# Top-k attention followed by an ELU feed-forward: the first eight steps laid out again (mask, weight tiles, pairs of keys, first sums)

## The chip, the cores and the metric

The kernel runs on one core of a Trainium2 chip. A core has a matrix engine (TensorE, PE in the profile, with PEld for its weight loads), a vector engine (VectorE, DVE), an activation engine (ScalarE, ACT), a general engine (GpSimd, POOL) and a queue engine that issues transfers (SyncE, SP). Each works through its own instructions in order, and they wait for each other by semaphores. The metric is the device time of one execution in microseconds (us), as the median of several runs.

## The reference

Two parts follow each other: attention that keeps the 32 largest scores of each row, and a feed-forward with ELU. All is fp32. The weights of the feed-forward come as fp64 and are turned to fp32 on the chip.

```python
B, H, S, D = 8, 8, 576, 64
scores = (1 / sqrt(D)) * q @ k.transpose(0, 1, 3, 2)
kth = np.partition(scores, -32, axis=-1)[..., -32:-31]
scores = np.where(scores >= kth, scores, -1e9)
scores = scores - scores.max(-1, keepdims=True)
attn = np.exp(scores)
attn = attn / (attn.sum(-1, keepdims=True) + 1e-9)
x = (attn @ v).transpose(0, 2, 1, 3).reshape(4608, 512)
h = x @ w_in                                  # 512 x 2048
g = np.where(h > 0, h, np.exp(np.minimum(h, 0)) - 1)
out = g @ w_out                               # 2048 x 512
```

## The kernel before, in words

**Steps.** The attention is cut into 144 steps. A step takes 128 queries (a tile of tokens) of one batch and one pair of heads; the 64 rows that are left over in each batch are done two pairs at a time. Four steps make up one full tile of tokens, so steps 0 to 3 are the first tile, 4 to 7 the second. Within a step VectorE finds the 32nd largest score of each row: four rounds of "the eight largest" (`first_max`, L336, and `next_max`, L348), with three replacements between them (L342) that put the found ones out of the way, each for two heads. This is the *selection*.

**Around the selection**, for the steps before and after it:
- `transpose_qk` (L261): a pair's keys and queries are transposed on TensorE (L268, L276) and copied from the accumulators by ScalarE (L273, L281) to a tile `kq`. `load_qk` (L216) brings the pair in by SP's queue, `keep_kq` (L283) writes the transposed pair to memory, and `load_kq` (L287) reads it back for later steps. There are 32 pairs, numbered through the batches; pairs 0 to 3 belong to batch 0.
- `scores` (L294): two halves of products on TensorE (L311), each copied by ScalarE (L331).
- the mask: in early steps (`mask_early`, L364) one tiny operation on VectorE (`field`, L374), four on GpSimd (L377 to L381), two Relus on ScalarE (L386), two subtractions on GpSimd (L389) and then `neg` (L355); in later steps (`mask`, L357) three GpSimd operations for each head (L360 to L362).
- `exp` (L392): two exponentials on ScalarE (L398) that also sum each row.
- `trans` (L427): the result is transposed on TensorE (L438, L456) and copied by ScalarE (L443, L457); `attend` (L459) multiplies by the values on TensorE (L471), and after a tile's last step ScalarE copies the sums out (L481).
- `sums` and `invert` (L403 to L425): after a tile's last step, three small operations on VectorE (L407 to L409) turn the sums over, and six transfers on SP's queue spread them over the partitions; then `normalise` (L483) multiplies on GpSimd (L486).

**The feed-forward** of finished tiles is cut into pieces, which `feed` hands to TensorE between the steps (L506 and L530), with ScalarE (L520 to L522) and GpSimd (L523) in between. How much it hands out follows from a list of due steps. What is left after step 143 runs alone at the end.

**The weights.** Both weight matrices come as 32 tiles of 128 x 512 fp64 numbers. `load_weights` brings them into borrowed places (L175): tiles of the feed-forward's `g`, spare tiles, and the part of `w_out` not yet written. `split_weight` does two ScalarE operations (L185, L186), `join_weight` two on VectorE (L191, L192) and an addition on GpSimd (L196). `weight_slot` (L203) does, for slot i, the join of tile i-2, the loads that may now be issued, and the split of tile i. `decode(n, place)` says at which places of step n there is a slot. Places 1, 3 and 5 lie in the middle of a round, between replacements and maxima; 2, 4 and 6 lie after the maxima. Two slots run ahead of step 0, four in each step, and six in steps 4 and 5, so that the last joins fall into step 6.

**The order** is written out by hand: the engines get their instructions in the order in which the loop over n calls these functions, with a step's own selection (`now`), the mask, exponentials and products of the step before (`last`), and the scores of steps to come. Steps 0 to 5 are *early*. There the mask of the step before is called first, at the start of step n; the scores of step n+2 in steps 0 to 3 and those of both 6 and 7 in step 4. At the end of step 3 three pairs (4, 5, 6) are transposed, at the end of step 4 two (7, 8), at the end of step 5 one (9), and from then on one in every second step. The sums of the first tile are called after place 4 of step 4, with a call of `load_weights`.

Of the kernel before, what the change touches and what calls it, by code (L numbers as in the profile page):

```python
# [61 lines left out]
def kernel(  # L62
# [81 lines left out]
    loads = [(0, 3, "g", -1), (3, 1, "raw", -1), (4, 3, "g", -1), (7, 1, "raw", -1)]  # L144
    loads += [(8, 4, "w", -1), (12, 4, "w", -1), (16, 3, "g", 2), (25, 1, "raw", -1)]
    loads += [(26, 1, "raw", -1), (27, 1, "raw", 3), (19, 3, "g", 6)]
    loads += [(28, 1, "raw", 7), (22, 3, "w", 15), (29, 1, "raw", 25)]
    loads += [(30, 1, "raw", 26), (31, 1, "raw", 27)]
    places_in_w_out = {8: 0, 12: 8, 22: 10}

    turn = [0]

    def load_weights(most=NW, margin=1):

        while loads and most > 0 and (
# [4 lines left out]
            if home == "w":  # L160
                at = places_in_w_out[i]
                t = w_out[:, at : at + 2 * n, :].bitcast(U32)
                t = t.rearrange("p (c f) d -> p c (f d)", f=2)
            elif home == "g":
                t = gpool.tile([P, n, 2 * WN], U32, tag="g", name="raw")[:]
            else:
                t = spare_tile(1 + turn[0] % 4, "raw")[:, 0 : 2 * WN].bitcast(U32)
                t = t.rearrange("p (c n) -> p c n", c=1)
                turn[0] += 1
# [46 lines left out]
    def load_qk(b, hp):  # L216

        first = b == 0 and hp < 3
        aside = (b, hp) in ((0, 1), (0, 2), (1, 1), (1, 2), (2, 0))
# [273 lines left out]
    def ffn_pieces(blk):  # L493
# [31 lines left out]
        def project(s, part):  # L525
# [11 lines left out]
            if part == 7:  # L537
# [11 lines left out]
                max(f // 4 * NC + NC - 1, 18 if f < NG else 21),  # L549
# [74 lines left out]
    def decode(n, place):  # L624

        if place in ((1, 2, 3, 4, 5, 6) if n in (4, 5) else (3, 4, 5, 6)):
            weight_slot()
# [8 lines left out]
    extra = {3: (4, 5, 6), 4: (7, 8), 5: (9,)}  # L636
    fetch = {2: (4, 5, 6), 3: (7, 8), 4: (9,), 5: (10,)}
    for p, pair in enumerate(pairs):
        if p >= NHP:
            n = next((n for n in extra if p in extra[n]), None)  # L640
            if n is None:
                n = EARLY + 1 + 2 * (p - 10)
                turns[n] = pair
            at(n + 1, keep_kq, *pair)
        elif p >= 2:
            at(p - 1, keep_kq, *pair)

    direct = {n: (n + 2,) for n in range(NHP)}
    direct[NHP] = (EARLY, EARLY + 1)
# [4 lines left out]
    for b in range(1, B):  # L654
        for hp, n in enumerate((-5, -4, 2, 2)):
            at(first[b] + n, load_v, b, hp)

    with tc.manual_schedule():
# [17 lines left out]
        for n in range(NS + 4):  # L676
# [7 lines left out]
            if early:  # L684
                if last:
                    mask_early(last)
                if n + 2 < NHP:
                    transpose_qk(0, n + 2)
                for m in direct.get(n, ()):
                    hp = m % NHP  # L690
                    steps[m].kq = {hp: kqT[0, hp]}
                    for half in range(2):
                        scores(steps[m], half)
# [11 lines left out]
            if n in turns:  # L705
                transpose_qk(*turns[n])
            if n >= EARLY and n + 2 in turns:
                load_qk(*turns[n + 2])
            if now and n > 0:
                first_max(now)  # L710
            if last and not early:
                biases(last, early)
                mask(last, 0)
            if early:
# [9 lines left out]
                feed(n, 0.5)  # L724
                next_max(now, (n, 3))
                decode(n, 4)
                if last and last.ends:
                    load_weights(margin=0)
                    sums(last)
# [16 lines left out]
            if last:  # L746
                mask(last, 1)
                exp(last, 0)
# [50 lines left out]
```

## Time and profile before

| what | value |
|---|---|
| median of 3 runs | 1663.88 us (1662.92 to 1664.91) |
| the profiled execution | 1664.04 us, span 1662.3 us |
| busy: PE, DVE, POOL, ACT | 1571.1, 1455.5, 1142.7, 925.7 us |
| start of step 1, 2, 3, 4 on VectorE (first L336) | 26.25, 42.62, 57.69, 72.79 us |
| start of step 5, 6, 7, 8 | 96.29, 118.04, 134.42, 144.07 us |

```profile
span 1662.3 us, 28290 instructions
## 2 busy tenths in 40 slices
PE   5559999999999999999999999999999999999999
...
DVE  6889999999999999999999989979989989987000
...
PEclk7579999999999999999999999999999999999999
DMA  9853555444453513121212321221222312210000
```

Each character is one slice of 41.6 us: the busy share in tenths, for PEclk the TensorE clock that was granted, for DMA the mean busy share of the transfer engines. The first three slices are the stretch that the change touches. In the last three VectorE has no work left, and TensorE does what remains of the feed-forward.

### The profile page before, as it was taken

The page shows a single profiled execution, that of the slowest core. Times are in us where ns is not written, and L with a number is a line of the kernel's source. Part 1 is how long each engine was busy: PE and PEld are TensorE (multiplying, and loading weights), DVE is VectorE, ACT ScalarE, POOL GpSimd, SP SyncE. Part 2 cuts the span into 40 slices and gives each one's busy share as a digit, 9 for nine tenths or more (in the row PEclk, how much of TensorE's full clock was granted, in tenths as well). Part 3 has the DMA queues.
Part 4 walks back from the last instruction along what each step waited for, and adds up shares of the span by engine and source line. Part 5 has one row for each costly group of instructions (what it writes and reads, how often), then busy time and mean ns, then how long its engine had stood idle before and what let it go on. Part 6 is the DMA issues. An engine that isn't in the chain of part 4 may idle for free.

```text
span 1662.3 us, 28290 instructions
## 1 busy us (share of the span) xinstructions
PE 1571.1 (95%) x9792; PEld 1046.9 (63%) x9792; DVE 1455.5 (88%) x3070; ACT 925.7 (56%) x1887; POOL 1142.7 (69%) x1457
## 2 busy tenths in 40 slices
PE   5559999999999999999999999999999999999999
PEld 3346777777776775757566566566556566566565
DVE  6889999999999999999999989979989989987000
ACT  6666665656665564646465476466456466355121
POOL 3567777777777786878778678668668668668021
PEclk7579999999999999999999999999999999999999
DMA  9853555444453513121212321221222312210000
GB/s 316 243 192 117 166 182 154 151 127 142 143 169 93 190 46 110 65 84 70 85 70 100 112 88 61 77 85 64 91 70 100 112 59 90 77 42 8 26 7 13
DMA packets 138895, 174.49 MB, mean 105 GB/s; under 512 B 94208, under 2 KB 102400, under 8 KB 138752
## 3 DMA queue, kind: packets, MB, share of 16 engines
q1 hardware_dynamic: 135200, 171.80, 32.3%
q8 instruction: 78, 1.28, 0.3%
q10 hardware_dynamic: 3552, 0.89, 0.3%
q14 instruction: 65, 0.53, 0.1%
HBM read 144.18 MB, written 28.46 MB: 104 GB/s over the span
## 4 chain that ended last, share of the span: by engine, by line
PE 60%; DVE 24%; POOL 5%; issue 4%; ACT 4%; DMA 2%; SPq 1%; ACTq 0%; POOLq 0%; DVEq 0%
PE ops L530 21%; PE hps L506 19%; DVE m L348 11%; DVE wk L342 10%; PE scps L311 7%; PE avps L471 6%; PE eps L438 5%; DVE m L336 2%; POOL sc L362 1%; POOL gT L523 1%; PE qkps L268 1%; ACT sc L398 1%; POOL wk L360 1%; POOL wk L361 1%; DMA rb<-recd 1%
## 5 line engine op out<-in xcount | busy, mean ns | idle before, releaser
L348 DVE MAX8 m<-wk 128x8 f32<-128x576 f32 x864 | 609.5, 747 | 0.0
L506 PE MATMUL hps<-xT,w_in 128*128 128x128 f32 (+2 forms) x2432 | 531.4, 373 | 10.4 <-ACT gT L521 5.8
L530 PE MATMUL ops<-w_out,gT 128*128 128x512 f32 x1152 | 519.6, 596 | 7.6 <-ACT osb L539 7.6
L506 PEld LDWEIGHTS hps<-xT,w_in 128*128 128x128 f32 x2432 | 381.1, 192 | 134.8 <-issue 17.7
L342 DVE MATCH_REPLACE8 wk<-m,wk 128x576 f32<-128x576 f32 x576 | 423.4, 743 | 0.0
L362 POOL TENSOR_TENSOR sc<-sc,wk 128x576 f32<-128x576 f32 x278 | 392.6, 1412 | 23.3
L398 ACT ACTIVATE sc<-sc,neg 128x576 f32<-128x576 f32 x288 | 224.0, 778 | 251.0 <-POOL sc L362 245.1
L530 PEld LDWEIGHTS ops<-w_out,gT 128*128 128x128 f32 x1152 | 209.6, 190 | 240.9 <-issue 213.8
L523 POOL TENSOR_TENSOR gT<-gT,n 128x384 f32<-128x384 f32 (+1 forms) x168 | 187.6, 1124 | 178.2 <-ACT n L522 174.2
L360 POOL TENSOR_SCALAR wk<-sc,nth 128x576 f32<-128x576 f32 x278 | 208.0, 748 | 27.0
L311 PE MATMUL scps<-kq 64*128 64x288 f32 (+3 forms) x1344 | 187.1, 428 | 31.2 <-ACT kq L273 20.7
L342 DVE MATCH_REPLACE8 wk<-m,sc 128x576 f32<-128x576 f32 x288 | 211.7, 743 | 0.0
L336 DVE MAX8 m<-sc 128x8 f32<-128x576 f32 x288 | 201.2, 740 | 11.3 <-ACT sc L331 11.1
L331 ACT COPY sc<-scps 128x576 f32<-128x576 f32 x288 | 170.0, 639 | 73.8 <-PE scps L311 71.9
L361 POOL TENSOR_SCALAR wk<-wk 128x576 f32<-128x576 f32 x278 | 185.7, 668 | 23.0
L443 ACT COPY et<-eps 128x1024 f32<-128x1024 f32 x144 | 144.5, 1003 | 90.6 <-PE eps L438 89.7
L471 PE MATMUL avps<-et,vE 128*64 128x128 f32 (+1 forms) x3200 | 179.6, 268 | 5.3 <-ACT et L443 5.3
L471 PEld LDWEIGHTS avps<-et,vE 128*64 128x64 f32 x3200 | 161.7, 139 | 32.3 <-issue 24.8
L438 PEld LDWEIGHTS eps<-ident,sc 128*128 128x128 f32 x1152 | 135.3, 142 | 72.3 <-issue 36.6
L438 PE MATMUL eps<-ident,sc 128*128 128x128 f32 x1152 | 153.2, 276 | 21.8 <-ACT sc L398 19.6
L311 PEld LDWEIGHTS scps<-kq 64*128 64x128 f32 (+1 forms) x1344 | 104.6, 180 | 103.1 <-issue 31.3
L520 ACT ACTIVATE n<-hps 128x384 f32<-128x384 f32 (+1 forms) x168 | 90.3, 537 | 108.8 <-PE hps L506 102.8
(66 smaller groups left out, 927.6 us busy)
## 6 DMA issues: line engine op xcount, KB each, us to landing
kq<-kqd SPq DMA_DIRECT2D x152, 576.0 KB
kqd<-kq SPq DMA_DIRECT2D x32, 576.0 KB
rb<-recd SPq DMA_DIRECT2D x64, 128.0 KB
out_dram<-osb SPq DMA_DIRECT2D x32, 256.0 KB
kin<-in_k_dram SPq DMA_DIRECT2D x27, 256.0 KB
qin<-in_q_dram SPq DMA_DIRECT2D x26, 256.0 KB
w_out<-in_moe_w_in_dram SPq DMA_DIRECT2D x2, 2048.0 KB
vE<-in_v_dram SPq DMA_DIRECT2D x32, 128.0 KB
```

The costliest lines, as they stand in the source:

```text
L311: nc.tensor.matmul(ps[rows, j, at : at + keys.stop - keys.start], u.kq[hp][r, 1, q0 : q0 + g.ql], u.kq[hp][r, 0, keys], start=True, stop=True,
L336: nc.vector.max(u.m1[:, i, :], u.sc[:, i, :])
L342: nc.vector.match_replace(u.wk[:, i, :], u.m[:, i, :], u.cur[:, i, :], TAKEN)
L348: nc.vector.max(u.m[:, i, :], u.cur[:, i, :])
L360: nc.gpsimd.tensor_scalar(pen, s, u.nth[:, i : i + 1], 2.0**100, ALU.add, ALU.mult)
L362: nc.gpsimd.tensor_tensor(s, s, pen, ALU.add)
L398: nc.scalar.activation(s, s, AF.Exp, bias=u.neg[:, i : i + 1], scale=scale, accum_out=g.den[:, at : at + 1],)
L438: nc.tensor.transpose(ps[:, i, c * P : (c + 1) * P], e[:, k0 + c * P : k0 + (c + 1) * P], ident[:],)
L471: nc.tensor.matmul(g.av[r, hp, 0:ql], vE[g.b, hp][:, i, (c + i) % (J + 1), :], u.et[:, at, q0 : q0 + ql], start=(c == 0), stop=(c == J),)
L506: nc.tensor.matmul(ps[:, f % G, :], w_in[:, i, f * P : (f + 1) * P], blk.xT[:, i, 0:N], start=(i == 0), stop=(i == NC - 1),)
L523: nc.gpsimd.tensor_tensor(g, g, n, ALU.subtract)
L530: nc.tensor.matmul(blk.o[:], blk.gT[f // NG][:, f % NG, s * P : (s + 1) * P], w_out[:, f, :], start=(f == 0), stop=(f == NF - 1),)
```

## The change

It does five things, all in the first eight steps:
- **The mask** of an early step is called at the end of that step's selection, ahead of its last join (place 6) and of any transposes there, instead of at the start of the step after. Step 5, too, now has the early kind of mask.
- **Weight tiles:** five slots in steps 4 and 5 instead of six (place 1 falls out), so that the last two joins fall into step 7. The list of loads and their places is another: more single tiles, tiles 21, 23, 25 and 27 in places of `w_out`, each spare tile named.
- **Pairs of keys:** one pair is transposed in a step, pairs 4, 5, 6 at the ends of steps 3, 4, 5, then pairs 7 to 11 in steps 7 to 11, then one in every second step. Each pair is loaded just after the pair before it was transposed, always to the same two buffers.
- **Scores** of step n+2 are called in each of the steps 0 to 5.
- **The first tile's sums** are called after place 2 of step 4, ahead of the third round, instead of after place 4, ahead of the fourth; the call of `load_weights` beside them is gone.

```diff
-    loads = [(0, 3, "g", -1), (3, 1, "raw", -1), (4, 3, "g", -1), (7, 1, "raw", -1)]
-    loads += [(8, 4, "w", -1), (12, 4, "w", -1), (16, 3, "g", 2), (25, 1, "raw", -1)]
-    loads += [(26, 1, "raw", -1), (27, 1, "raw", 3), (19, 3, "g", 6)]
-    loads += [(28, 1, "raw", 7), (22, 3, "w", 15), (29, 1, "raw", 25)]
-    loads += [(30, 1, "raw", 26), (31, 1, "raw", 27)]
-    places_in_w_out = {8: 0, 12: 8, 22: 10}
+    loads = [(0, 3, "g", -1), (3, 1, 1, -1), (4, 3, "g", -1), (7, 1, 2, -1)]
+    loads += [(8, 4, "w", -1), (12, 4, "w", -1), (16, 2, "g", 2), (20, 1, 1, 3)]
+    loads += [(18, 2, "g", 6), (22, 1, 2, 7), (24, 1, 3, -1), (26, 1, 4, -1)]
+    loads += [(21, 1, "w", 12), (23, 1, "w", 13), (25, 1, "w", 14), (27, 1, "w", 15)]
+    loads += [(28, 1, 1, 20), (29, 1, 2, 22), (30, 1, 3, 24), (31, 1, 4, 26)]
+    places_in_w_out = {8: 0, 12: 8, 21: 8, 23: 10, 25: 12, 27: 14}
...
-                t = spare_tile(1 + turn[0] % 4, "raw")[:, 0 : 2 * WN].bitcast(U32)
+                t = spare_tile(home, "raw")[:, 0 : 2 * WN].bitcast(U32)
...
-        aside = (b, hp) in ((0, 1), (0, 2), (1, 1), (1, 2), (2, 0))
+        aside = (b, hp) in ((0, 1), (0, 2))
...
-                max(f // 4 * NC + NC - 1, 18 if f < NG else 21),
+                max(f // 4 * NC + NC - 1, 17 if f < NG else 19),
...
-        if place in ((1, 2, 3, 4, 5, 6) if n in (4, 5) else (3, 4, 5, 6)):
+        if place in ((2, 3, 4, 5, 6) if n in (4, 5) else (3, 4, 5, 6)):
...
-    extra = {3: (4, 5, 6), 4: (7, 8), 5: (9,)}
-    fetch = {2: (4, 5, 6), 3: (7, 8), 4: (9,), 5: (10,)}
     for p, pair in enumerate(pairs):
         if p >= NHP:
-            n = next((n for n in extra if p in extra[n]), None)
-            if n is None:
-                n = EARLY + 1 + 2 * (p - 10)
-                turns[n] = pair
+            n = p - 1 if p < NHP + 3 else p
+            n = n if n < EARLY + 5 else EARLY + 5 + 2 * (n - EARLY - 5)
+            turns[n] = pair
             at(n + 1, keep_kq, *pair)
...
-    direct = {n: (n + 2,) for n in range(NHP)}
-    direct[NHP] = (EARLY, EARLY + 1)
...
+    coming = [turns[n] for n in sorted(turns)]
+
+    def load_next():
+        if coming:
+            load_qk(*coming.pop(0))
...
             if early:
-                if last:
-                    mask_early(last)
                 if n + 2 < NHP:
                     transpose_qk(0, n + 2)
-                for m in direct.get(n, ()):
-                    hp = m % NHP
-                    steps[m].kq = {hp: kqT[0, hp]}
-                    for half in range(2):
-                        scores(steps[m], half)
+                ahead = steps[n + 2]
+                ahead.kq = {hp: kqT[0, hp] for hp in ahead.hps}
+                for half in range(2):
+                    scores(ahead, half)
...
-            if n in turns:
+            if n in turns and not early:
                 transpose_qk(*turns[n])
-            if n >= EARLY and n + 2 in turns:
-                load_qk(*turns[n + 2])
+                load_next()
             if now and n > 0:
                 first_max(now)
-            if last and not early:
+            if last and n > EARLY:
                 biases(last, early)
                 mask(last, 0)
...
                 if last:
                     trans(last)
                 feed(n, 0.5)
+                if last and last.ends:
+                    sums(last)
                 next_max(now, (n, 3))
                 decode(n, 4)
-                if last and last.ends:
-                    load_weights(margin=0)
-                    sums(last)
                 if last:
                     attend(last)
                 next_max(now, (n, 5))
-                decode(n, 6)
                 if last and last.ends:
                     normalise(last.g)
-                for p in extra.get(n, []):
-                    transpose_qk(*pairs[p])
-                for p in fetch.get(n, []):
-                    load_qk(*pairs[p])
+                mask_early(now)
+                decode(n, 6)
+                if n in turns:
+                    transpose_qk(*turns[n])
+                if n >= NHP - 2:
+                    load_next()
                 continue
...
             if last:
-                mask(last, 1)
+                if n > EARLY:
+                    mask(last, 1)
                 exp(last, 0)
```

Built, the orders of VectorE, ScalarE, GpSimd, TensorE and SP differ from those before in steps 0 to 10 alone, but for the places of later pairs and their transfers.

More of the change, by code (lines that the diff above doesn't have):

```diff
@@ L137, in weight @@
         return w_out[:, i - NF, :]
-    loads = [(0, 3, "g", -1), (3, 1, "raw", -1), (4, 3, "g", -1), (7, 1, "raw", -1)]
-    loads += [(8, 4, "w", -1), (12, 4, "w", -1), (16, 3, "g", 2), (25, 1, "raw", -1)]
-    loads += [(26, 1, "raw", -1), (27, 1, "raw", 3), (19, 3, "g", 6)]
-    loads += [(28, 1, "raw", 7), (22, 3, "w", 15), (29, 1, "raw", 25)]
-    loads += [(30, 1, "raw", 26), (31, 1, "raw", 27)]
-    places_in_w_out = {8: 0, 12: 8, 22: 10}
-    turn = [0]
+    loads = [(0, 3, "g", -1), (3, 1, 1, -1), (4, 3, "g", -1), (7, 1, 2, -1)]
[4 more added lines that the diff above has]
+    places_in_w_out = {8: 0, 12: 8, 21: 8, 23: 10, 25: 12, 27: 14}
     def load_weights(most=NW, margin=1):
@@ L166, in load_weights @@
             else:
-                t = spare_tile(1 + turn[0] % 4, "raw")[:, 0 : 2 * WN].bitcast(U32)
+                t = spare_tile(home, "raw")[:, 0 : 2 * WN].bitcast(U32)
                 t = t.rearrange("p (c n) -> p c n", c=1)
-                turn[0] += 1
             if i < NF:
```

## The prediction

> **What bounds the kernel now.** I read first how busy the engines are in stretches of 20 us. Columns: stretch, its length, busy time (and instructions) of PE, weight load, VectorE (DVE), ScalarE (ACT), GpSimd (POOL), then TensorE's clock, DMA share, GB/s.
>
> ```profile
> 80.00:100.00 20.00, 12.81 (x68) 9.01 (x69) 12.49 (x29) 16.61 (x31) 12.64 (x12) 0.67 0.72 236
> 100.00:120.00 20.00, 11.00 (x82) 9.80 (x80) 17.67 (x29) 11.98 (x22) 14.05 (x16) 0.76 0.43 145
> 140.00:160.00 20.00, 17.35 (x88) 9.76 (x88) 20.00 (x43) 11.83 (x25) 16.24 (x21) 1.00 0.14 33
> 240.00:260.00 20.00, 20.00 (x142) 13.43 (x142) 19.93 (x44) 13.34 (x28) 15.74 (x19) 1.00 0.45 132
> ```
>
> From 140 on VectorE is full, and from 240 TensorE too: there is nothing to win there but an earlier start. Before that VectorE stands still, and the timeline of VectorE says for whom (start, duration, instruction, then the idle time before it and who ended it):
>
> ```profile
> 63.24 1.15 DVE L191 TENSOR_SCALAR w_in<-w_in 128x512 uint32<-128x512 uint32 x1
> 75.57 0.41 DVE L191 TENSOR_SCALAR w_out<-w_out 128x512 uint32<-128x512 uint32 x1
> 87.60 0.43 DVE L191 TENSOR_SCALAR w_out<-w_out 128x512 uint32<-128x512 uint32 x1 [7.31 <-ACT w_out L185]
> 107.28 0.54 DVE L191 TENSOR_SCALAR w_out<-w_out 128x512 uint32<-128x512 uint32 x1 [2.27 <-ACT w_out L185]
> ```
>
> In step 4 a join waits 7.31 us for ScalarE's split, in step 5 2.27 us. The chain of waits shows what held ScalarE up in step 4 (start, us, what):
>
> ```profile
> 73.20 0.90 ACT kq L273
> 74.14 1.98 PE qkps L268 x8
> 76.15 1.02 ACT kq L273
> 77.21 1.98 PE qkps L268 x8
> 79.22 1.02 ACT kq L273
> 80.28 4.53 PE scps L311 x16
> 84.84 0.64 ACT sc L331
> 85.48 1.52 ACT sc L398 x4
> 87.00 0.56 ACT w_out L185
> ```
>
> Three pairs are transposed in turn, TensorE and ScalarE waiting for each other, then two steps' scores, then the exponentials, and only then the split. Last, the mask and its surroundings:
>
> ```profile
> 45.30 1.63 ACT L386 ACTIVATE wk<-sc,pos,nth 128x576 f32<-128x576 f32 x2 [2.29 <-POOL pos L381]
> 49.42 0.78 ACT L398 ACTIVATE sc<-sc,neg 128x576 f32<-128x576 f32 x1 [1.44 <-POOL neg L355]
> 99.25 5.49 PE L506 MATMUL hps<-xT,w_in 128*128 128x128 f32 x24 [1.36 <-POOL xT L486]
> ```
>
> **Does a gain before 144 us reach the end?** From step 8 (144.07) to step 80 VectorE's steps are 9.6 to 10.3 us, with a few up to 11.2, and scores are copied 16 to 28 us before VectorE reads them. The orders of all five engines are the same there but for one pair of keys, transposed a step or two later. So the start of step 8 is what counts; later steps shift with it. TensorE has 26.5 us idle between the starts of steps 4 and 11, into which a shift of some 10 us fits.
>
> **The change, part by part.** Step starts before (first L336): 26.25, 42.62, 57.69, 72.79, 96.29, 118.04, 134.42, 144.07 for steps 1 to 8. VectorE's prices: two maxima 1.33 (26.25 to 27.58), two replaces 1.44 (27.58 to 29.02), so a bare step is 4 x 1.33 + 3 x 1.44 = 9.64; a join 0.93 (75.57 to 76.50); sums 0.56 (91.03 to 91.59); field 0.08. ScalarE's: a split 1.13 (53.47 to 54.60); the two relus 1.53 (45.30 to 46.83); from the first copy of a pair to the end of the exponentials behind it 5.54 (30.48 to 36.02). Below S is the start of a step on VectorE.
>
> *Mask sooner, steps 1 to 3.* The field now stands ahead of the last join, at S-1.0. GpSimd's small operations take 0.94 (44.36 to 45.30), with 0.2 to notice; the relus start at S+0.15, not S+2.7 (45.30 against 42.62), end at S+1.7, and the split that was ahead of them ends at S+2.8. L389 and L355 need 4.1 after the relus' start (45.30 to 49.42), so the exponentials start at S+4.3, not S+6.8. In steps 2 and 3 this covers the wait of 0.55 for a split, and L389 is over at S+3.9, before the first join at S+5.5, which beside it took 1.15 and not 0.41: 0.55 + 0.74 = 1.3 less, twice. Step 1 has a pair to copy: exponentials end at S+2.8+5.54 = S+8.35 (before, S+9.8), so the late join goes from S+12.84 to S+11.4: 1.4 less. Sum -4.0. If no wait goes, 0; if all of step 1's does, -5.2. The join's add (L196) now queues behind the mask on GpSimd; only a weight load far behind waits for it.
>
> *Step 4: one pair, one step's scores, five tiles, sums sooner.* Two pairs (6.16, from 73.06 to 79.22) and one step's scores (2.2, from 82.62 to 84.84) leave the chain. ScalarE: S+2.8, then 5.54: exponentials end at S+8.35. VectorE gets to the sums after 1.33 + 1.44 + 1.33 + 0.93 = 5.03 and waits 3.3 there: the change puts a new wait one round ahead of where the sums stood before. Behind it stand all of VectorE's later rounds; later splits (ending S+9.5 and S+11.9) are then in time. Step: 9.64 + 5 x 0.93 + 0.56 + 0.08 + 3.3 = 18.25 against 23.50: -5.25. With TensorE at full clock throughout (eight scores 1.24, not 2.29) -6.3; with exponentials at S+11, -2.6.
>
> *Step 5: five tiles.* GpSimd has the normalise (1.27, L486) ahead of the mask's operations, as before: relus 1.1 later, exponentials end at S+9.45. TensorE ends the scores at S+3.9+3.3 (30.48 to 33.81) = S+7.2, then the 24 L506 at 5.49, eight transposes 1.7: S+14.4. ScalarE: copies 1.07, L520 to L522 1.49, half a split 0.57: S+17.55. Before, two splits stood ahead of this; now one does, so the fourth join, due at S+11.1, waits 6.45. Step: 9.64 + 4.65 + 0.08 + 6.45 = 20.8 against 21.75: -0.95. Ends: L506 at full clock (20 took 2.40) -3.5; two more us of lag +1.1.
>
> *Step 6.* Four joins as before, but the selection's late mask (six operations on GpSimd, L360 to L362) is replaced by the early one, over before the first join. Of 3.0 us by which joins were stretched beside GpSimd (16.38 - 9.64 - 4 x 0.93), I keep 0.9: 14.3, -2.1; ends 0 and -3.0.
>
> *Step 7.* Two joins that were elsewhere: 1.86, and 0.4 of stretch: +2.3; ends +1.9 and +4.0 (each beside an add, as at 132.71: 1.78 for 0.68).
>
> *At nothing.* Loads: four more issues on SP (0.34 to 0.55 each); tiles 28 to 31 are asked for two to five slots ahead. The last load before took 3.43 and held ScalarE 4.60 with VectorE full; cover gone, it costs that. Pairs at steps 8 to 11 are loaded one step ahead, not two: four issues take 2.85 (152.15 to 155.00), landing at most 4.5 (the first load of q), 7.4 against a step of 9.6; cover gone, 1 to 3 us of TensorE, with scores 18 us ahead. I take 0, worst +2.
>
> Sum: -4.0 - 5.25 - 0.95 - 2.1 + 2.3 = **-10.0**. The profiled execution took 1664.04 (span 1662.3), the median is 1663.88: **1654.0**.
>
> [...]
>
> **Rivals.** (1) *Slower: ScalarE stays late and the early sums wait for it.* One mechanism, at L407 in step 4 and the fourth join in step 5. For it: exponentials ended at S+14.1 in step 4 before and ScalarE was busy 16.61 of 20 there. Against: 8.4 us of that chain are gone. If they end at S+14.1 in both steps, step 4 is 14.1 + 9.9 = 24.0, step 5 20.8 + 4.65 = 25.4, the mask gains nothing in steps 1 to 3 and 6, step 7 keeps +2.3: 1664.0 + 0.5 + 3.7 + 2.3 = 1670.5. It decides from 5 us more lag in each of both steps. (2) *Hidden: TensorE holds the time.* For it: 20.00 of 20 from 240 on, so an earlier VectorE could only stand further behind. Against: its waits before 173, one of 9.2 at 121.66 and 3.6 in step 10. Then 1661 to 1664. (3) *Waits only change place:* step 4 as at exponentials S+11, step 5 and 6 unchanged, the mask half: -2.0 - 2.6 + 2.3 = -2.3, 1661.7.
>
> **How the numbers follow.** Forecast 0.72, (1) 0.10, (2) 0.08, (3) 0.10. Without (1), the sums' ends are put together so that not all go one way: 1648 to 1662, which leaves out (1), part of (2), and a little below. What a measurement can tell from no change is about 0.2%, 3.3 us, so 1660.6 to 1667.2 is "same". Faster: 0.72 and a third of (2) and (3), 0.78; slower: most of (1), 0.09; same 0.13.
>
> **What would show it.** Right: step 8 starts near 134; VectorE waits some 3 us at L407 in step 4 and some 6 at the fourth join of step 5, for ScalarE both times; no join of steps 2 and 3 above 0.5 for L191; step 7 near 12. Wrong: a wait of 8 at L407, step 8 earlier and the end not, or a load that ends ScalarE's wait in step 6.

## The result and the profile after

The kernel after takes 1660.83 us in the median of 20 runs (1659.07 to 1663.1), the kernel before on the same chip 1663.59 (1660.33 to 1666.02): a ratio of 0.9985, 95% interval 0.9978 to 0.9992. It is faster, by some 2.5 us where 10 were forecast. The profiled execution after has a span of 1659.9 us, against 1662.3 before. A line number after is that of before less 3.

Step lengths on VectorE, in us, from one first maximum to the next, against the forecast:

| step | before | after | change | forecast |
|---|---|---|---|---|
| 0, with its start | 26.25 | 26.83 | +0.6 | 0 |
| 1, 2, 3 | 16.37, 15.07, 15.10 | 15.46, 13.72, 13.71 | -3.65 | -4.0 |
| 4 | 23.50 | 19.92 | -3.6 | -5.25 |
| 5 | 21.75 | 21.30 | -0.45 | -0.95 |
| 6 | 16.38 | 14.10 | -2.3 | -2.1 |
| 7 | 9.65 | 12.77 | +3.1 | +2.3 |
| step 8 starts at | 144.07 | 137.82 | **-6.25** | -10.0 |
| 8 to 11 | 39.1 | 39.1 | 0 | 0 |
| 12 | 9.65 | 12.24 | **+2.6** | 0 |
| 13 | 10.2 | 11.13 | **+0.9** | 0 |
| step 14 starts at | 203.0 | 200.3 | -2.7 | -10.0 |

The rest of the run follows step 14: step 143 starts 2.7 us sooner, and TensorE's last matmul ends 2.7 sooner (1658.5, then 1655.8). So there are two losses: 3.75 us on the way to step 8, and 3.5 in steps 12 and 13, far behind the change. Of the first loss 0.6 lies in step 0 and is taken for scatter: the five other variants here whose steps 0 to 8 are those of after have 13.8 to 15.4 us in step 0 and start step 8 at 136.8 to 137.9.

Busy time in stretches of 20 us of after (columns as in the prediction):

```profile
80.00:100.00 20.00, 10.88 (x58) 9.00 (x59) 19.96 (x38) 12.73 (x23) 12.50 (x13) 0.60 0.44 137
100.00:120.00 20.00, 11.24 (x84) 8.55 (x83) 16.85 (x32) 12.30 (x21) 12.61 (x14) 0.74 0.47 135
140.00:160.00 20.00, 19.76 (x76) 11.00 (x74) 19.93 (x44) 9.23 (x19) 16.11 (x23) 0.83 0.53 149
160.00:180.00 20.00, 18.52 (x166) 15.79 (x162) 18.31 (x37) 12.61 (x25) 11.43 (x14) 1.00 0.75 219
```

The 7.5 us that VectorE stood still from 80 to 100 are gone there (a new wait of 3.60 ends just before, at 78.51), from 100 to 120 some remain, and from 160 to 180 VectorE now stands still for 1.7 us where it had 19.93 of 20 before. TensorE has 19.76 of 20 from 140 on (17.35 before), in part at half clock: 0.83 instead of 1.00.

The waits and the stretched instructions on VectorE's timeline after (start, duration, instruction, idle time before it and who ended it):

```profile
78.51 0.17 DVE L404 TENSOR_SCALAR den<-den 128x8 f32<-128x8 f32 x1 [3.60 <-ACT sc L395]
87.56 1.24 DVE L371 TENSOR_SCALAR field<-m 128x2 uint32<-128x2 uint32 x1
...
96.20 1.30 DVE L188 TENSOR_SCALAR w_out<-w_out 128x512 uint32<-128x512 uint32 x1
...
104.93 1.05 DVE L188 TENSOR_SCALAR w_out<-w_out 128x512 uint32<-128x512 uint32 x1 [3.12 <-ACT w_out L182]
105.90 1.78 DVE L189 SCALAR_TENSOR_TENSOR raw<-raw 128x512 uint32<-128x512 uint32 x1
...
130.96 1.89 DVE L189 SCALAR_TENSOR_TENSOR raw<-raw 128x512 uint32<-128x512 uint32 x1
...
180.80 0.09 DVE L339 MATCH_VALUE_LOAD wk<-m,sc 128x8 f32 x1 [2.49 <-POOL sc L359]
...
198.78 1.09 DVE L404 TENSOR_SCALAR den<-den 128x8 f32<-128x8 f32 x1
```

The first row is the new wait that the prediction put into step 4, before the sums. The 2.49 us at 180.80 are the loss in step 12, and they are no wait for scores: the replacement wants to write `wk`, of which there are two buffers, and the one it gets is still being read by the late mask of step 10 (L359). The last row is step 13's loss: an operation on 8 elements a row that took 0.15 at the end of step 9 (157.09).

GpSimd's timeline after shows why that mask was late:

```profile
169.51 1.42 POOL L359 TENSOR_TENSOR sc<-sc,wk 128x576 f32<-128x576 f32 x1
176.39 1.28 POOL L520 TENSOR_TENSOR gT<-gT,n 128x512 f32<-128x512 f32 x1 [5.46 <-ACT n L519]
177.78 0.75 POOL L357 TENSOR_SCALAR wk<-sc,nth 128x576 f32<-128x576 f32 x1
178.61 0.67 POOL L358 TENSOR_SCALAR wk<-wk 128x576 f32<-128x576 f32 x1
179.36 1.41 POOL L359 TENSOR_TENSOR sc<-sc,wk 128x576 f32<-128x576 f32 x1
```

The mask's second half stands in GpSimd's queue behind the gate of the feed-forward (L520), which waits for ScalarE and that for TensorE's products (L503). The last 32 of these ahead of the gate started at 171.28; before, at 173.20. VectorE came 6.25 us sooner, TensorE only 1.9.

The chain of waits, before, in the same stretch:

```profile
162.02 1.41 DVE m L348 x2
164.01 0.75 POOL wk L360
...
170.09 1.28 POOL xT L486
171.42 0.71 PE hps L506 x4
172.13 0.87 PE qkps L268 x8
173.27 3.77 PE hps L506 x32
```

and after:

```profile
137.89 0.67 DVE m L333
...
139.35 0.78 PE scps L308 x4
...
140.90 1.97 PE qkps L265 x8
142.87 0.40 PE qkps L273 x2
143.27 3.71 PE ops L527 x4
...
149.92 0.88 PE qkps L265 x8
150.80 0.26 PE qkps L273 x2
...
164.09 1.11 PE qkps L265 x8
...
166.29 0.58 PE eps L435 x4
166.87 3.52 DMA qin<-in_q_dram
170.43 0.66 PE qkps L265 x4
171.09 0.27 PE qkps L273 x2
171.35 3.77 PE hps L503 x32
```

Before, the chain runs through VectorE's selections to 163.4 and passes to TensorE at 171.42. After, it leaves VectorE at 138.6 and from there on is TensorE's work, item after item, but for ScalarE's copies between them and one load. Two things tell the cause. Transposes of pairs (L265, L273) in steps 8 and 10 were not there before. And from 140.5 to 147.3 TensorE's clock was granted at half: four output products (L527) took 3.71 instead of 1.9 there, and the pair of step 8 took 2.37 where that of step 9 took 1.14.

Between the gate's first ScalarE instruction in step 7 and that in step 11, 35.5 us passed before and 40.6 after, 5.1 more. TensorE's time between them, by operation: transposes of pairs 2.5 before, 6.3 after (+3.9, two pairs more, one of them at half clock); output products 12.5 and 14.1 (+1.6, the same 28 matmuls); all else +0.2; idle 5.1 and 4.4 (-0.6). So the pairs and the clock are mixed in these sums; the runs below separate them.

### The profile page after: what moved, and what is told of

Read it like the earlier page. It is cut to its first block, busy times and chain, and to the rows that moved or that the text cites. A ratio compares the mean times of both kernels' runs of the same rounds, so it can differ in the third digit from the quotient of the medians.

```text
span 1659.9 us, 28307 instructions
## 1 busy us (share of the span) xinstructions
PE 1572.5 (95%) x9792; PEld 1047.9 (63%) x9792; DVE 1454.2 (88%) x3071; ACT 927.4 (56%) x1889; POOL 1143.4 (69%) x1456
## 4 chain that ended last, share of the span: by engine, by line
PE 69%; DVE 19%; ACT 4%; issue 3%; POOL 2%; DMA 2%; SPq 1%; ACTq 0%; POOLq 0%
PE ops L527 24%; PE hps L503 22%; DVE m L345 8%; PE scps L308 8%; DVE wk L339 8%; PE avps L468 8%; PE eps L435 5%; DVE m L333 2%; PE qkps L265 1%; DMA kq<-kqd 1%; POOL sc L359 1%; DMA qin<-in_q_dram 1%; ACT sc L395 1%; PE eps L453 1%; ACT sc L328 1%
## 5 line engine op out<-in xcount | busy, mean ns | idle before, releaser
L503 PE MATMUL hps<-xT,w_in 128*128 128x128 f32 (+2 forms) x2432 | 530.7, 372 | 5.7 <-ACT gT L518 5.7
L527 PE MATMUL ops<-w_out,gT 128*128 128x512 f32 x1152 | 521.4, 598 | 7.1 <-ACT osb L536 7.1
L503 PEld LDWEIGHTS hps<-xT,w_in 128*128 128x128 f32 x2432 | 380.6, 192 | 130.1 <-issue 18.5
L359 POOL TENSOR_TENSOR sc<-sc,wk 128x576 f32<-128x576 f32 x276 | 389.5, 1411 | 23.1
L527 PEld LDWEIGHTS ops<-w_out,gT 128*128 128x128 f32 x1152 | 210.0, 190 | 240.6 <-issue 214.6
L520 POOL TENSOR_TENSOR gT<-gT,n 128x384 f32<-128x384 f32 (+1 forms) x168 | 188.0, 1127 | 195.6 <-ACT n L519 192.8
```

The lines of the kernel that those rows point to most:

```text
L359: nc.gpsimd.tensor_tensor(s, s, pen, ALU.add)
L503: nc.tensor.matmul(ps[:, f % G, :], w_in[:, i, f * P : (f + 1) * P], blk.xT[:, i, 0:N], start=(i == 0), stop=(i == NC - 1),)
L520: nc.gpsimd.tensor_tensor(g, g, n, ALU.subtract)
L527: nc.tensor.matmul(blk.o[:], blk.gT[f // NG][:, f % NG, s * P : (s + 1) * P], w_out[:, f, :], start=(f == 0), stop=(f == NF - 1),)
```

## The theories and the experiments

- **V**, the prediction's: the start of step 8 on VectorE decides.
- **T**: TensorE has no room in steps 8 to 11; the two more pairs make it late, and this reaches VectorE through the gate, GpSimd's queue and `wk`.
- **C**: the stretch of half clock from 140.5 (6.8 us long) makes it late.
- **W**: the one wait for `wk` is the loss; without it VectorE's gain stays.

Every variant was timed in 5 rounds beside the kernel before. They ran on several chips, on which the kernel before had medians of 1662.98 to 1663.71, so the ratios compare better than the medians. Many of the intervals overlap that of after; the steps in the profiles tell more than the medians of such variants. The column "gate" is the time between the two ScalarE instructions named above; "wait" is VectorE's in step 12; the next two say how much sooner than before VectorE starts steps 14 and 72 in the profiled execution.

| kernel | median us | ratio (95%) | step 8 | gate | wait | step 14 | step 72 |
|---|---|---|---|---|---|---|---|
| after | 1660.83 | 0.9985 (0.9978-0.9992) | 137.8 | 40.6 | 2.49 | 2.7 | 2.7 |
| e1_pairs_second | 1659.06 | 0.9982 (0.9973-0.9991) | 136.6 | 39.0 | 0.96 | 5.5 | 5.3 |
| e2_sums_back | 1660.09 | 0.9984 (0.9976-0.9993) | 136.4 | 40.4 | 2.34 | 4.3 | 4.3 |
| e3_six_tiles | 1658.20 | 0.9972 (0.9962-0.9982) | 135.4 | 36.9 | 1.27 | 5.8 | 5.8 |
| e4_mask_only | 1664.44 | 1.0009 (1.0-1.0018) | 143.8 | 33.9 | none | -0.3 | -0.3 |
| e5_wk3 | 1658.56 | 0.9975 (0.9966-0.9984) | 136.8 | 40.7 | none | 6.6 | 6.9 |
| e6_warm | 1660.49 | 0.9990 (0.9981-0.9998) | 137.9 | 39.3 | 1.20 | 3.9 | 3.5 |
| e7_mask_first | 1661.98 | 0.9992 (0.9984-1.0001) | 137.0 | 40.6 | none | 5.7 | 3.5 |
| e8_both | 1657.65 | 0.9970 (0.9960-0.9981) | 134.1 | 36.3 | 0.64 | 7.8 | 6.7 |
| e9_wk3_once | 1659.34 | 0.9981 (0.9972-0.9990) | 137.0 | 40.7 | none | 6.5 | 3.3 |
| e10_before_wk3 | 1662.82 | 0.9994 (0.9985-1.0002) | 143.9 | 35.5 | none | 0.2 | 1.1 |
| e11_all | 1657.96 | 0.9965 (0.9953-0.9977) | 135.6 | 36.2 | none | 7.8 | 6.3 |
| e12_before_pe | 1663.58 | 0.9999 (0.9990-1.0008) | 141.2 | 36.2 | none | 2.8 | 3.1 |
| e13_after_pe | 1663.99 | 1.0002 (0.9993-1.0011) | 137.0 | 43.3 | 5.22 | 0.8 | 0.8 |
| e14_both_back | 1660.73 | 0.9988 (0.9979-0.9997) | 136.4 | 36.4 | 0.77 | 5.3 | 4.3 |

### One part undone, or done alone

**e1_pairs_second**: after, with pairs from the eighth on in every second step (7, 9, 11, ...), so that steps 8 and 10 have none.

```diff
-            n = p - 1 if p < NHP + 3 else p
-            n = n if n < EARLY + 5 else EARLY + 5 + 2 * (n - EARLY - 5)
+            n = p - 1 if p < NHP + 3 else EARLY + 1 + 2 * (p - NHP - 3)
```

> The changed kernel, but from step 7 on a pair of keys is transposed in every second step (7, 9, 11 and on) instead of in each of 7 to 11. Theory T (TensorE is held up by the transposes that were moved to steps 8 and 10, and its lag makes VectorE wait in step 12): step 8 starts near 137.8 as in the changed kernel, the wait of 2.5 us in step 12 and the 0.9 us of step 13 go, time about 1657.5. Theory C (the half-speed stretch of TensorE's clock around 141 to 148 us makes the lag, not the transposes): the half-speed stretch and at least 2 of the 3.4 us stay, time about 1660. Theory V (what decides is the start of step 8 on VectorE): no difference from the changed kernel, 1660.8.

The wait in step 12 falls from 2.49 to 0.96, and step 14 starts 5.5 us sooner than before, not 2.7 (0.76 of that difference is step 0's scatter). The gate's stretch shrank from 40.6 to 39.0. As much half clock lay in it as in after (two stretches of 3.4 us, from 138.8 and 166.1, for one of 6.8), so the two pairs alone are worth some 1.5 us, in the stretch and in the wait (TensorE is busy for 2.3 us less there and idle for 0.8 more). That speaks for T, for a part of the loss; the end (1659.06, ratio 0.9982) is not clear of that of after.

**e2_sums_back**: after, with the first tile's sums behind place 4 again.

```diff
                 feed(n, 0.5)
-                if last and last.ends:
-                    sums(last)
                 next_max(now, (n, 3))
                 decode(n, 4)
+                if last and last.ends:
+                    sums(last)
```

> The changed kernel, but the first tile's sums are called where they were before, a round later. Theory V (VectorE's waits in steps 4 to 7 decide): the wait of 3.6 us for the exponentials at the sums in step 4 goes, of which a later join may take back up to 1; step 8 starts 2.5 to 3.6 us sooner (134 to 135.3), time about 1658. Theory T or C (TensorE holds the time from step 8 on): step 8 starts sooner by as much, but VectorE waits longer in step 12; time within 0.7 us of 1660.8.

Step 4 falls to 16.0 us and step 5 rises to 24.3: together 40.3, against 41.2 after. With five tiles the earlier sums are worth nothing by step 8. What it has gained by step 14, 4.3, it loses in part further on: half clock is granted for 3.4 us from 770.6, and TensorE comes out of that 2.6 us sooner than before.

**e3_six_tiles**: after, with six tiles in steps 4 and 5.

```diff
-        if place in ((2, 3, 4, 5, 6) if n in (4, 5) else (3, 4, 5, 6)):
+        if place in ((1, 2, 3, 4, 5, 6) if n in (4, 5) else (3, 4, 5, 6)):
```

> The changed kernel, but six weight tiles in steps 4 and 5 as before, so the last joins fall into step 6 and not 7. If five tiles are worth what the prediction said (two splits ahead of the wait for the feed-forward in step 5 are lost, joins in step 7 cost 2.3): step 4 is 0.9 longer, step 5 about 1.5 shorter, step 7 3.1 shorter, step 6 as it was: step 8 starts near 134. Theory C in particular: with no adds in step 7 GpSimd is free sooner, ScalarE and TensorE don't wait there (2.1 and 2.7 us), the clock doesn't drop, and the time falls to about 1657. Theory T: 1659.5 to 1660.8, VectorE waiting longer in step 12.

Step 4 is 20.7 (+0.8), step 5 21.5, step 7 9.7 (-3.1): the sixth tile goes into waits that are there anyway (0.42 at the sums instead of 3.60, 1.01 at the fourth join instead of 3.12). No stretch of half clock lies between 122 and 626, the gate's stretch is 36.9, and the wait in step 12 is 1.27. TensorE has the same 221 instructions in that stretch as in after, the two more pairs among them, and is busy for 33.3 us with them instead of 36.1. So at full clock the two pairs make the stretch 1.4 longer than before (35.5); the other 3.7 of after's 5.1 go with the half clock, as theory C expected. It comes with the five tiles: all seven kernels here with five tiles and nothing put ahead of step 8's scores have a fall between 138.8 and 140.5 (after, e1, e2, e5, e7, e9, e13), none of the four variants of after with six tiles has (e3, e8, e11, e14), nor has before. With five tiles the change thus pays 3 us for its two joins in step 7, and again for the clock behind them.

**e4_mask_only**: the kernel before, with the mask alone at the end of the selection, in step 5 too.

```diff
             if early:
-                if last:
-                    mask_early(last)
...
                 if last and last.ends:
                     normalise(last.g)
+                mask_early(now)
+                decode(n, 6)
```

> The kernel before, with the mask at the end of the selection as the only part of the change (step 5 masked the early way too). Theory V: steps 1 to 3 lose 0.9, 1.4 and 1.4 us and step 6 some 2 as in the changed kernel, step 0 gains up to 0.8; step 8 starts near 139 to 140 and the time is about 1659. Theory T or C: the pairs lie as before, so nothing of this is lost behind step 8; the same 1659. If it gains under 1 us, the mask's part of the gain comes only together with the other parts.

Steps 1 to 3 gain what they gain in after (15.5, 13.7, 13.7), and steps 4 and 5 give it all back (26.4 and 24.7): step 8 starts at 143.8. Its chain of waits shows how for step 5:

```profile
91.76 1.16 DMA recd<-recT
...
97.63 1.27 POOL xT L486
...
99.96 0.27 POOL pos L381
...
101.03 0.85 ACT wk L386
101.88 0.55 ACT w_out L185
```

The mask of step 4 stands on GpSimd behind the normalise (L486), which waits for the sums' transfers. The Relus start at 100.26, 4.8 us into step 5, not 0.6 as in after. There the sums come sooner, and the normalise is over at 88.77, ahead of step 5 (89.64).

**e14_both_back** takes the sums back in the fastest version (e8, below), where their wait was 0.42.

> The kernel after with pairs spread over every second step, six tiles in steps 4 and 5, and the first tile's sums back behind place 4, as in the kernel before. With six tiles VectorE waited only 0.42 us at the early sums, so if their place matters through that wait alone the start of step 8 is 133.5 to 134.1 as without it and the median 1657 to 1658. If sooner sums help otherwise (later waits), step 5 is longer by 1 to 3 us and the median 1658.5 to 1660.

"Through that wait alone" is wrong: step 4 falls by 2.4, step 5 rises from 20.8 to 24.9, and the median from 1657.65 to 1660.73. The Relus start 4.4 us into step 5 instead of 0.6. So the earlier sums are worth some 3 us where six tiles fill the wait before them, and nothing where they don't (e2).

### The wait in step 12

**e5_wk3**: after, with a third buffer for `wk` in every third step from 12 on. **e9_wk3_once**: in step 12 alone (`if u.n == 12`). **e10_before_wk3**: the edit of e5 on the kernel before.

```diff
-        size = ((2 * J + 2) * P, 2 * S, 2 * WN)[i // 2]
+        size = ((2 * J + 2) * P, 2 * S, 2 * S)[i // 2]
...
-        u.wk = wkpool.tile([P, 2, S], FP32, tag="wk", name="wk")
+        if u.n >= 12 and u.n % 3 == 0:
+            u.wk = spare_tile(4, "wk").rearrange("p (i s) -> p i s", i=2)
+        else:
+            u.wk = wkpool.tile([P, 2, S], FP32, tag="wk", name="wk")
```

> The kernel after with a third buffer for wk: from step 12 on every third step takes it, so that the selection of step 12 no longer writes the buffer that the late mask of step 10 still reads. Order of work on every engine as in after. Theory W (the gain is lost because VectorE waits for that one buffer): step 12 falls from 12.2 us to 9.7, nothing comes in its place, span 1659.9 - 2.5 = 1657.4. Theory T (TensorE is behind and VectorE would be held by the next thing that hangs on it, the late mask of step 11 or the scores): step 12 9.7, but the 2.5 us appear in steps 13 to 15, span 1659.5 to 1660.

> The kernel after with the third buffer for wk in step 12 alone (in the run before it was taken by every third step from 12 on, and the waits of steps 81 and 91 went too). Theory W: the 4.3 us of that run came from steps 12 and 13 alone; VectorE starts step 14 some 6.6 us sooner than in the kernel before (2.7 in the kernel after), holds that to step 72, and the end follows: span 1655.5 to 1656, or 1657.5 if a stretch of half clock falls near 770 again. Theory T (TensorE's lateness in steps 8 to 11 sets the end whatever VectorE does): span 1659.5 to 1660.

> The kernel before with the third buffer for wk in every third step from 12 on. Theory W: before has no such wait ahead of step 81, so step 72 starts at the same time; steps 81 and 91 fall by some 4 us each, but TensorE has no idle time left there and the end stays: span 1662 to 1662.6. Rival (the buffer is worth 4 us of its own, in the late steps): span 1658.

In e5 step 12 is 9.6 us, step 14 starts 6.6 sooner, and the end comes 6.7 sooner. In e9, too, step 14 starts 6.5 sooner, but step 23 is 2.1 longer and step 33 0.8. VectorE's one wait in between, and what GpSimd was doing:

```profile
288.20 0.09 DVE L342 MATCH_VALUE_LOAD wk<-m,sc 128x8 f32 x1 [1.96 <-POOL sc L362]
```

```profile
283.80 1.28 POOL L523 TENSOR_TENSOR gT<-gT,n 128x512 f32<-128x512 f32 x1 [3.47 <-ACT n L522]
285.18 0.75 POOL L360 TENSOR_SCALAR wk<-sc,nth 128x576 f32<-128x576 f32 x1
286.01 0.67 POOL L361 TENSOR_SCALAR wk<-wk 128x576 f32<-128x576 f32 x1
286.76 1.41 POOL L362 TENSOR_TENSOR sc<-sc,wk 128x576 f32<-128x576 f32 x1
```

It is the same wait, eleven steps later. VectorE was further ahead of TensorE than two buffers allow, TensorE itself had gained little more than in after (2.6 us at the gate of step 11, for 1.9), and what VectorE had gained went at the next such place; W alone falls. In e5 the third buffer lets VectorE keep its lead. TensorE stays 2.6 to 4.0 us sooner until 604, and by 697 it is 6.9 sooner, having caught up where it stands idle in the other kernels (between 600 and 700 us it is idle 3.7 us in after, 1.3 in e5). From 780 on all ends with TensorE: e5's steps 81 and 91 are 4 us shorter each, step 143 starts 12.0 sooner, and the end only 6.7. e10 agrees: its steps 81 and 91 fall by 3.5 and the end does not move.

**e7_mask_first**: in step 11 the second half of the mask is issued ahead of the gate.

```diff
                 mask(last, 0)
+                if n == 11:
+                    mask(last, 1)
...
-                if n > EARLY:
+                if n > EARLY and n != 11:
                     mask(last, 1)
```

> The kernel after, but in step 11 the second half of the late mask of step 10 is issued on GpSimd straight after the first half, ahead of the gate's subtraction that waits for ScalarE and TensorE; nothing else moves. Theory W (the in-order queue of GpSimd carries TensorE's lateness to VectorE): the late mask ends some 7 us sooner, step 12 9.7 instead of 12.2, and the gate 2.2 us later at most; span 1657.4. Theory T (TensorE itself holds the time): the wait returns in steps 13 to 15, span 1659.5 to 1660.

Step 12 is 9.6, and the wait returns: 0.93 us at 188.10, 0.46 at 199.14, longer steps 21 and 33, 3.5 left at step 40 of the 5.7 at step 14. As in e9, taking the wait away without giving TensorE time only moves it.

### TensorE's work and its clock

**e6_warm**, **e12_before_pe** and **e13_after_pe** add transposes of the identity, whose result nobody reads: 20 at the start of step 8 of after, ahead of the scores (e6), and 20 in each of steps 8 and 9 of before (e12) and of after (e13), behind the scores. The edit of e12 and e13:

```diff
+            if n in (8, 9):
+                idle = ps_h.tile([P, WN], FP32, tag="h", name="warm")
+                for _ in range(20):
+                    nc.tensor.transpose(idle[:, 0:P], ident[:], ident[:])
             decode(n, 0)
```

> The kernel after with 20 more 128x128 transposes of the identity on TensorE at the start of step 8 (some 1.5 to 2 us of work, result unused), put where TensorE was idle before its clock was granted at half for 6.8 us from 140.5. Theory C (the half clock there makes TensorE late, the four matmuls of the output projection took 3.8 us and not 1.9): the stretch is gone or shorter, the hidden sums x32 start 1 to 2 us sooner than 171.3, step 12 10 to 11 us instead of 12.2, span about 1658. Theory T (TensorE has simply more work there than time): the added work costs as much as the clock gives, step 12 12 to 13, span 1659.9 to 1661.

With the added work ahead of the scores the clock stays up in step 8. TensorE's timeline, in after and then in e6:

```profile
139.35 1.31 PE L308 MATMUL scps<-kq 64*128 64x288 f32 x8 [2.72 <-ACT sc L328]
...
143.20 3.78 PE L527 MATMUL ops<-w_out,gT 128*128 128x512 f32 x4
```

```profile
139.44 1.30 PE L308 MATMUL scps<-kq 64*128 64x288 f32 x8 [0.82 <-ACT sc L328]
...
142.27 1.98 PE L527 MATMUL ops<-w_out,gT 128*128 128x512 f32 x4
```

Twenty transposes more, and TensorE is 1.3 us faster over the stretch (39.3), the wait in step 12 1.20 instead of 2.49. So C holds: the half clock cost more than the added work does. The end gains nothing: the 1.2 us are lost where half clock is granted for 3.4 us from 771.6, with VectorE's lead 3.5 at step 72 and TensorE's 1.8 behind it. e2 and e7 lose 1.7 at the same place; after, e1, e3, e5 and e8 have no such stretch there.

> The kernel before with 20 more 128x128 transposes of the identity on TensorE in step 8 and 20 in step 9 (result unused; 2.0 us each by the run that had 20 of them), about what the moved pairs of keys put there (4.0 us). VectorE's work and the start of step 8 stay as they are. Theory T (TensorE's work in steps 8 to 11 reaches the end through the gate, GpSimd's queue and wk): the gate's first ScalarE instruction of step 11 comes at 180.6 instead of 176.6, a wait of 1.5 to 2.3 for the late mask appears in step 12, step 13 0.9 longer, span 1664.7 to 1665.5 (1.7 more if a stretch of half clock falls near 770). The prediction's claim (what counts is the start of step 8, and TensorE has room): no wait in step 12, span 1662.3.

Theory T's wait did not come here. On the kernel before, 4.5 us more of TensorE's work (143.51 to 145.75 and 151.40 to 153.64) moved the gate's stretch by 0.7 and the median not at all. TensorE in before, and then in e12, where step 8 starts 2.8 us sooner:

```profile
171.42 0.71 PE L506 MATMUL hps<-xT,w_in 128*128 128x128 f32 x4 [3.28 <-POOL xT L486]
```

```profile
169.40 0.61 PE L506 MATMUL hps<-xT,w_in 128*128 128x128 f32 x4
169.85 0.60 PE L268 MATMUL qkps<-ident,kin 128*128 128x128 f32 x4
```

Before, TensorE stood still in step 10 until GpSimd had normalised the second tile; the added work went into that wait. In after the tile is normalised sooner and the wait is gone, so the same edit was tried there:

> The kernel after with 20 more 128x128 transposes of the identity on TensorE in step 8 and 20 in step 9 (result unused, 2.0 us each). On the kernel before the same work cost nothing, where TensorE stood idle for 3.28 us in step 10 until GpSimd had normalised xT; in the kernel after that wait is gone. Theory T (after has no room left on TensorE in steps 8 to 11): the gate's first ScalarE instruction of step 11 comes 3 to 4 us later (less up to 1.8 if the added work keeps the clock from falling to half near 140), VectorE's wait in step 12 grows from 2.5 us by as much, to 4 to 6.5, and the median is 1662.5 to 1664.5. If TensorE has room there (the prediction's claim): 1660.8, as after.

```profile
182.68 0.09 DVE L339 MATCH_VALUE_LOAD wk<-m,sc 128x8 f32 x1 [5.22 <-POOL sc L359]
```

The wait in step 12 grows by 2.7 us and the median to 1663.99: the whole gain of the change is gone, for work on an engine in steps in which VectorE's own work is unchanged. That TensorE has no room there, and that its lateness reaches VectorE, is shown, and V falls: step 8 started at 137.0.

TensorE in the gate's stretch, in us, side by side:

| kernel | pairs | added work | half clock | busy | idle | gate |
|---|---|---|---|---|---|---|
| before | 2 | 0 | 0 | 30.4 | 5.1 | 35.5 |
| e12_before_pe | 2 | 4.5 | 0 | 34.4 | 1.8 | 36.2 |
| e8_both | 2 | 0 | 3.4 | 31.9 | 4.3 | 36.3 |
| e1_pairs_second | 2 | 0 | 6.8 | 33.8 | 5.3 | 39.0 |
| e3_six_tiles | 4 | 0 | 0 | 33.3 | 3.6 | 36.9 |
| e6_warm | 4 | 1.9 | 0 | 35.7 | 3.6 | 39.3 |
| after | 4 | 0 | 6.8 | 36.1 | 4.4 | 40.6 |
| e13_after_pe | 4 | 4.9 | 3.4 | 38.8 | 4.5 | 43.3 |

Of the 5.7 us that TensorE is busier in after than before, 2.9 are the two pairs (e3 against before) and 2.8 the half clock (after against e3). T and C both hold, each for about half of that, as far as one profiled execution of each kernel tells.

### The fastest version

**e8_both** puts e1 and e3 together, **e11_all** adds the third buffer.

> The kernel after with both variants that were faster: keys of the fifth pair on spread over every second step from step 7 on, and six tiles in steps 4 and 5. Start of step 8 at 134.0 to 134.5 (135.4 and 136.6 alone, of which 0.7 in step 0 and 0.4 in step 5 are the pairs'). Theory T/W: TensorE has fewer transposes in steps 8 to 11, so that step 12 is 9.7 to 11 and step 13 10.2 to 11.1: span 1654.5 to 1656.5. If the later waits are fixed in place (they end when TensorE is done, whenever VectorE came): step 12 grows by what step 8 starts sooner, span 1656.7 to 1657.2.

> The kernel after with everything that was faster: pairs spread over every second step, six tiles in steps 4 and 5, third buffer for wk. Theory W: the 0.6 us of wait left in step 12 goes, step 13 0.3 less as with the buffer alone, nothing else: span 1654.5 to 1655, TensorE's first sums after step 8 as without the buffer. Theory T: 1655.7, no change.

e8 starts step 8 at 134.1 and has 1657.65 us, 3.2 below after's median (by the ratios 2.5): the fastest median, and its end is 6.6 us before that of the kernel before in the profiles. The third buffer adds nothing to it that shows: 1657.96. The wait in step 12 goes, but step 8 had started 1.5 later in the profiled execution, and step 14 starts as in e8.

## Why the prediction was wrong

**The step that failed** is the passage under "Does a gain before 144 us reach the end?": "The orders of all five engines are the same there but for one pair of keys, transposed a step or two later. So the start of step 8 is what counts", with "TensorE has 26.5 us idle [...], into which a shift of some 10 us fits." It cost 3.5 us of the 7.3 that the forecast was off: 2.6 in step 12, which waits for `wk`, 0.9 in step 13, where the sums' first operation took 1.09 us beside GpSimd's late mask. What the runs showed in its place: TensorE is busier by 5.7 us in the gate's stretch and has 0.6 less idle to give.
- The count was wrong. The diff turns one pair in each of steps 7 to 11, where before had one in steps 7, 9 and 11. So steps 8 to 11, taken as unchanged, have two pairs more: 2.9 us of TensorE at full clock.
- The clock was put at nothing. Behind the two joins of step 7 TensorE waited 2.72 us for scores, and from 140.5 its clock was granted at half for 6.8 us: 2.8 us more for the same instructions. In before the clock was full from 126 to 900 us.
- The idle time was no room. TensorE took its work in the order given, and 21.9 of its 26.5 us idle lay in steps 4 to 7, above all in waits for ScalarE, ahead of that work. Between the starts of the same steps it was 28.3 us after, not less. The one idle that could take anything, 3.28 us in step 10, hung on the second tile's normalise and went as that came sooner.
- The way back was not seen. That "scores are copied 16 to 28 us before VectorE reads them" holds for the scores only. TensorE's lateness came by another way: gate, GpSimd's queue, late mask, `wk`.

**The other 3.75 us, up to step 8**, are sizes.
- *Mask sooner, steps 1 to 3*, -4.0: -3.65, right. The waits for L191 in steps 2 and 3 are gone. By itself it is worth nothing (e4: step 8 at 143.8). With the other parts it lasts, without the earlier sums too (e2: 136.4); which of them it needs is not shown. The term of 0.2 "to notice" is shown in no run: in after 0.09 passed from the field to GpSimd's first small operation (41.45 to 41.54). These operations took 1.32 instead of 0.94 (41.54 to 42.86), and the Relus started 0.57 into steps 2 to 4, not 0.15.
- *Step 4*, -5.25: -3.6. The mechanism is right, the wait 3.60 for 3.3. The term that was mis-sized is the field, put at 0.08: it took 1.24 (87.56 to 88.80), beside GpSimd's normalise (87.51 to 88.77).
- *Step 5*, -0.95: -0.45, from two errors that cancel. The fourth join waited 3.12, not 6.45. Instead four VectorE operations beside GpSimd's work on whole tiles (96.20, 104.93, 105.90 and the field at 109.04) took 3.5 more than alone (1.30, 1.05, 1.78 and 1.05 for 0.41, 0.41, 0.68 and 0.17).
- *Step 6*, -2.1: -2.3, right.
- *Step 7*, +2.3: +3.1, as one join (130.96) took 1.89 instead of 0.68.
- *At nothing*: the weight loads cost nothing, and no load holds ScalarE in step 6. Pairs loaded one step ahead were not quite hidden: TensorE waited 0.34 us for `qin` at 170.43, as steps 10 and 11 lie only 5 us apart on TensorE.

**The rivals.** The first (ScalarE late, sums waiting 8 us) did not come. The second, "TensorE holds the time", is what came, for 3.5 us of the forecast 10, though for other reasons than that TensorE is full from 240 on. Of the waits put against it, "9.2 at 121.66 and 3.6 in step 10", the one lies ahead of the stretch and the other goes when the normalise comes sooner. Of the signs named beforehand, "step 8 earlier and the end not" is the one that showed, in part: 6.25 us sooner and 2.7. The end lies within the range only by 1.2 us.

In three more places of after a VectorE operation took longer, each time beside GpSimd: the field at the normalise (1.24 for 0.17 in the steps before), a join in step 7 (1.89 for 0.68, which the prediction had only as an end of its range) and the sums of step 13 (1.09 for 0.15). The first operation of the first join in steps 2 and 3 took 0.49 and 0.48 us, where it had taken 1.14 and 1.15 before.

## What to carry to other kernels

When work is moved out of a crowded stretch, follow it to where it lands and ask what idle time that engine has there, in its own order; idle time ahead of that point is no room (here 21.9 of 26.5 us lay ahead). An engine's lead over another is bounded by the buffers between them (with two for `wk` VectorE waited 2.49 us in step 12, with a third not at all), so a gain on the leading engine must be followed through every buffer that it writes again, not only through the data that it reads. The parts of such a change should be tried alone and in pairs: here the mask gains nothing alone, the earlier sums gain only with six tiles, and two parts of the change (five tiles, a pair in each step) cost time: step 14 starts 3.1 and 2.8 us sooner without them. And the gap that the change opened on TensorE cost as much again, as its clock fell behind it (2.72 us idle, then 2.8 by the half clock).

## What the runs showed of the hardware

- TensorE's clock fell to half here in places where TensorE had not stood idle throughout. In after, it had worked 1.16 of the last 3.41 us ahead of the fall at 140.5 (3.41 us is the shortest stretch at one clock inside the span, in after as in before). Twenty falls lie between 120 and 900 us in fourteen of the sixteen profiled executions; TensorE had worked 0.71 to 1.81 us of the 3.41 us ahead of them, and each lasted 3.4 or 6.8 us. With work that nobody needs ahead of the gap the clock stayed full in step 8 (e6: four output products took 1.98 us at 142.27, against 3.78 in after); with such work behind the gap it fell at 139.9 (e13: eight transposes of a pair took 1.97 us at 140.06, and 0.87 at 149.64).
- A VectorE operation on 8 elements a row (L404, in after) took 1.09 us and ended as GpSimd's L359 did: 198.78 + 1.09 = 199.87, and L359 ran from 198.44 to 199.84. At 157.09, with GpSimd idle, it took 0.15. The maxima and replacements were not stretched: each took 0.72 to 0.76 us in before and after, whatever GpSimd did beside it.
- One profiled execution can mislead by 3 us in these steps: in e12, whose first eight steps are those of before, step 4 took 21.4 us instead of 23.5, with stretches of half clock at other places, and the span was 1659.1, while the median was that of before.
